# Moving the first small transfers of a decode kernel from SyncE's queue to ScalarE's

## The chip, the cores and the metric

The kernel runs on one core of a Trainium2 chip. The metric is device microseconds (us) of one execution. Before the change three runs took 1076.17, 1074.54 and 1074.22 us; their median is 1074.54 us.

The engines are called as in the profile: PE is TensorE (PEld its weight loads), DVE is VectorE, ACT is ScalarE, POOL is GpSimd, SP is SyncE. Each engine works off its own instructions in order. A transfer from the chip's memory is issued by an instruction on SP or on ACT; each of the two has a queue of transfers of its own (SP's is q1 in the profile, ACT's is q10), and the core's 16 DMA engines serve both.

## The reference

The kernel computes one decode step, for 8 batch rows of width 448, of two attention blocks with two MLP blocks between and behind them:

```python
x = x + A(layernorm(x))     # attention over cached keys and values
x = x + B(layernorm(x))     # MLP block
x = x + A(layernorm(x))     # the same weights and caches again
x = x + B(layernorm(x))

# A: 16 query heads on 8 cached heads, 4096 cached positions, head width 256
q = (x @ wq) as [8, 16, 1, 256]
p = softmax(q @ k^T / 16)
return (p @ v) as [8, 1, 4096] @ wo

# B: with one position only; the shifted groups are zero
x1 = x + shifted(gelu(layernorm(x) @ w1)) @ w2   # = x for one position
return x1 + gelu(layernorm(x1) @ w3) @ w4
```

With a sequence of one position each of the four shifts of `hs` reads only padding, so that part of B adds nothing and w1 and w2 are never loaded. The caches are 8 batch rows x 8 heads x 4096 positions x 256 numbers in bf16, 2 MB for the keys of one row and head and 2 MB for its values: 128 MB of each. They do not fit on the chip and are read for each of the two attention blocks, but for what is kept in between. In all the profile counts 434.18 MB read.

## The kernel before

**Storage.** Keys and values lie in 30 slots of 512 KB (`kv`, `QUARTERS = 30`); one row and head of keys is four units of one slot each. One SP transfer brings one to four consecutive units, that is 512 KB to 2 MB. The weights lie beside them and stay. The 448 rows of `wq` and of `w3` do not divide by 128, so their last 64 rows are folded: `wqx_sb` holds the left half of the columns on partitions 0 to 63 and the right half on partitions 64 to 127 (256 KB each), `w3x_sb` the same for the MLP (112 KB each). The input row lies in `x_row`: the 448 columns, and once more the last 64 of them.

**Work on one row and head.** `front`: PE transposes the keys of each unit (L1510), DVE or ACT moves the result from PSUM back over the keys (L1441, L1442), PE multiplies with the queries (L1406 or L1149), then the softmax. `back`: PE multiplies the probabilities with the values (L1276), DVE splits the sum in two bf16 parts, and PE multiplies with `wo` (L1340). When the last unit of a load has been read, its slots come free.

**Beginning.** `first_queries` transposes the input row on PE (L1600), normalises it (`norm`, L847 and L851 on PE, then a chain on DVE), and multiplies with `wq_sb` and `wqx_sb` (L902 in `q_mms`). Scores of the first head wait for that. The transposes of the first keys do not.

**Loops.** Batch rows run in order; the first attention of row b+1 overlaps the second attention of row b. Keys of five heads and seven value units stay in their slots from the first attention of a row to the second. The MLP of each row (`mid`) stands between its two attentions; that of the first six rows' second block runs once for all of them, that of the last two at the end.

**What sets the order.** All work is first described as operations with their readers and writers (`Plan.op`). `Plan.schedule` then assigns each engine its order by a list scheduling with modelled times: of what is ready, the least `prio` goes first; PE's time depends on how many columns the last window of 3.413 us had (`WIN`, `COLS`), filler matmuls (L1719) are put into gaps of PE from 20 us on. SP's operations go strictly by `prio`; keys and values count up from 0 (`loads`), and a load given `at` gets `4 * at - 0.5`. The planner takes 0.45 us for an issue on SP and starts a transfer 4.0 us after its issue or when the one ahead is done:

```python
free[e] = t + 0.45
start = max(t + self.ISSUE, dma_end)
dma_end = start + o.dur
```

For keys and values it also decides, at that modelled time, which slots are taken and how many units go in one transfer (`next_kv`); single places cap this (`MOST = 1` for the values of three heads of the rows 1 to 7 in the first attention). On ACT a transfer counts 0.1 us and is taken to be there at once. The order and the waits that follow are then written out for each engine; nothing is decided on the chip.

**The first transfers.** On SP: the input row in two pieces (`at` 0), the left half of `wqx` (0.05), the left half of `w3x` (0.06), two key transfers of 2 MB, then `wq` in three pieces of 1 MB (`at` 2), values and keys, `wo`. On ACT: the right halves of `wqx` (L1576) and `w3x` (L1580), then the load of its function table, then nothing until the first eviction.

Of the kernel before, what the change touches and what calls it, by code (L numbers as in the profile page):

```python
# [6 lines left out]
P = 128  # L7
B = 8
D = 448
# [467 lines left out]
def bass_interleave_layers__gqa_block_cached__mixer_s_mlp__decode_kernel(  # L477
# [20 lines left out]
    plan = Plan()  # L498
# [6 lines left out]
    def sb(name, shape, dt):  # L505
        n = 4 if dt in (f32, i32) else 2
        for s in shape[1:]:
            n *= s
        al = 32 if n >= 128 else 8
        cursor[0] = (cursor[0] + al - 1) // al * al  # L510
        t = nc.alloc_sbuf_tensor_at(name, shape, dt, offset=cursor[0], align_bytes=al)
        cursor[0] += (n + al - 1) // al * al
        assert cursor[0] <= high0, (name, cursor[0], high0)
        return t

    wq_sb = sb("wq_sb", [P, 3, 4096], bf)
    wqx_sb = sb("wqx_sb", [P, 2048], bf)
    wo_sb = sb("wo_sb", [P, 32 * D], bf)
    w3_sb = sb("w3_sb", [P, 3, F], bf)
    w3x_sb = sb("w3x_sb", [P, F // 2], bf)  # L520
# [40 lines left out]
    def over(name, shape, dt, at, skip=0):  # L561
        return nc.alloc_sbuf_tensor_at(name, shape, dt, offset=at.manual_sbuf_range[0] + skip)
# [13 lines left out]
    x_row = over("x_row", [B, NC5 * P], bf, w4_sb)  # L576
# [49 lines left out]
    def dma(name, dst, src, nbytes, sem, val, wr, at, row=8192):  # L626

        us = nbytes / 16 / 26.88e3 + nbytes / row / 16 * 0.008
        plan.op("sp", lambda eng: eng.dma_start(dst, src), us / FASTER, name, wr=wr, prio=at,  # L629
                dma=(sem, val))  # L630

    def dma_once(name, parts, keys, at, also=()):

        for i, (dst, src, nbytes, *row) in enumerate(parts):
            dma(name, dst, src, nbytes, nc.alloc_semaphore(f"s_{name}{i}"), 16,
                [keys[i], *(also if i == 0 else ())], 4 * at - 0.5, *row)
# [49 lines left out]
    def const_c(v):  # L686
# [7 lines left out]
            wr=["sel"])  # L694
# [7 lines left out]
    for bank, key in [(psR, "R"), (psM, M)]:  # L702
        plan.op("dve", lambda v, bank=bank: v.memset(bank[:, :], 0.0), 0.5, "const",
                wr=["psM", ("row", 0), ("row", 1)], banks=[key])
# [851 lines left out]
    def second_queries(b, h, prio):  # L1556
# [8 lines left out]
           rd=["psM", ("mom2", b), "cs_q"], wr=[("q2", b % 2, h)], banks=[M], prio=prio)  # L1565


    dma_once("x", [(x_row[:, 0:D], A_x[:, 0, :], 7168), (x_row[:, D + P:], A_x[:, 0, 3 * P:D], 1024)],
             ["xr0", "xr1"], 0)

    def load_wq():
        dma_once("wq", [(wq_sb[:, kc, :], A_wq[kc * P:(kc + 1) * P, :], 1 << 20)
                        for kc in range(3)], ["wq0", "wq1", "wq2"], 2)
        dma_once("wqx", [(wqx_sb[0:64, :], A_wq[384:D, 0:2048], 1 << 19)], ["wqx0"], 0.05)
        s_wqx = nc.alloc_semaphore("s_wqx1")
        plan.op("act", lambda a: a.dma_start(wqx_sb[64:P, :], A_wq[384:D, 2048:4096]), 0.1, "wqx1",  # L1576
                wr=["wqx1"], prio=0, dma=(s_wqx, 16))
        dma_once("w3x", [(w3x_sb[0:64, :], B_w3[384:D, 0:896], 114688)], ["w3x0"], 0.06)
        s_w3x = nc.alloc_semaphore("s_w3x1")
        plan.op("act", lambda a: a.dma_start(w3x_sb[64:P, :], B_w3[384:D, 896:1792]), 0.1, "w3x1",  # L1580
                wr=["w3x1"], prio=1, dma=(s_w3x, 16))

    def load_rest():
        dma_once("wo", [(wo_sb[:, :].rearrange("p (t n) -> p t n", n=2 * D),
# [68 lines left out]
    def with_first_results(k, b):  # L1653
# [15 lines left out]
        run(k[MLP_TO:])  # L1669

    load_wq()
    load_rest()
    first_queries()
# [105 lines left out]
```

## Time and profile before

| | |
|---|---|
| median of three runs | 1074.54 us (1074.22 to 1076.17) |
| the profiled execution | 1071.74 us |
| its span, first to last instruction | 1069.8 us |
| busy: PE, DVE, ACT, POOL | 937.8, 586.8, 345.6, 99.6 us |
| mean granted clock of PE | 0.954 |
| bytes moved, mean rate | 436.39 MB, 408 GB/s |
| first instruction on SP and ACT | 0.72 us |
| first key transfer issued, landed | 2.89, 12.27 us |
| last values landed | 1059.96 us |
| issues of 512 KB: values, keys | 174, 29 |
| issues of 2 MB: values, keys | 61, 66 |

The shares of busy time are means over the span. The page's DMA row shows in tenths how much of each fortieth of the span the 16 DMA engines were in transfer; the GB/s tell how much they moved in it, so that a busy engine with little moved can be seen. "SPq" and "ACTq" are the instructions that issue transfers on the two queues. The chain that ended last is followed back from the last instruction; a DMA piece in it begins at the issue and ends at the landing.

### The profile page before, as it was taken

How to read it: one execution, taken by the hardware profiler on the slowest of the kernel's cores; microseconds unless marked ns; L12 is line 12 of the kernel's file. 1: busy time of each engine (PE TensorE's matmuls, PEld its weight loads, DVE VectorE, ACT ScalarE, POOL GpSimd, SP SyncE). 2: the span in 40 equal slices, each digit the busy share in tenths (PEclk: the TensorE clock that was granted, in tenths of full speed). 3: DMA queues.
4: the chain of work that ended last, by engine and by line, in shares of the span. 5: the costliest groups of instructions: out<-in, count | busy, mean ns of one | idle time of the engine just before them, and what ended most of it. 6: DMA issues, size and time to landing. Idle time of an engine off the chain costs nothing.

```text
span 1069.8 us, 34153 instructions
## 1 busy us (share of the span) xinstructions
PE 937.8 (88%) x15215; PEld 650.7 (61%) x15215; DVE 586.8 (55%) x1879; ACT 345.6 (32%) x946; POOL 99.6 (9%) x284
## 2 busy tenths in 40 slices
PE   4889889998989989988898888898888998998896
PEld 4556556665556656666565565666656675666664
DVE  4345455555555556555565555565555665665464
ACT  1234113341334502354133431344223342253041
POOL 0000000010100101001010100101000000111011
PEclk9899999999999989999999999999999998999896
DMA  9999999999999999999999999999999999999995
GB/s 364 409 425 424 408 391 426 424 422 404 406 427 424 420 396 419 426 426 418 385 424 424 422 403 386 426 425 425 397 402 425 427 419 387 407 425 416 381 422 229
DMA packets 58110, 436.39 MB, mean 408 GB/s; under 512 B 6238, under 2 KB 9452, under 8 KB 35948
## 3 DMA queue, kind: packets, MB, share of 16 engines
q1 hardware_dynamic: 57796, 433.84, 98.6%
q8 instruction: 119, 1.95, 0.7%
q10 hardware_dynamic: 168, 0.38, 0.1%
q14 instruction: 27, 0.22, 0.1%
HBM read 434.18 MB, written 0.01 MB: 406 GB/s over the span
## 4 chain that ended last, share of the span: by engine, by line
DMA 56%; PE 36%; DVE 4%; issue 2%; SPq 1%; ACT 1%; POOL 0%
DMA kv<-in_A_k_cache_dram 30%; DMA kv<-in_A_v_cache_dram 26%; PE psT L1510 11%; PE psP L1276 8%; PE psT L1406 5%; PE psM L1149 3%; PE psM L902 2%; PE psR L1340 2%; PE psP L1719 1%; SPq L629 1%; PE psM L918 1%; DMA w_sb<-in_B_w_dram 1%; DVE oS L1304 1%; DVE oS L1302 1%; PE psP L1312 1%
## 5 line engine op out<-in xcount | busy, mean ns | idle before, releaser
L1510 PE MATMUL psT<-ident_f,kv 128*128 128x128 f32 x2752 | 372.7, 282 | 27.9 <-DMA kv<-in_A_k_cache_dram 26.2
L1510 PEld LDWEIGHTS psT<-ident_f,kv 128*128 128x128 f32 x2752 | 301.5, 143 | 107.6 <-issue 56.6
L1441 DVE COPY kv<-psT 128x512 f32<-128x512 f32 x364 | 250.4, 691 | 186.4 <-PE psT L1510 179.2
L1442 ACT COPY kv<-psT 128x512 f32<-128x512 f32 x356 | 207.9, 586 | 376.3 <-PE psT L1510 300.3
L1276 PE MATMUL psP<-kv,pT 128*2 128x256 bf16 x4032 | 170.9, 281 | 26.3 <-DMA kv<-in_A_v_cache_dram 24.3
L1406 PE MATMUL psT<-kv,qz 128*32 128x512 bf16 x1664 | 134.2, 396 | 3.8 <-ACT kv L1442 1.9
L1276 PEld LDWEIGHTS psP<-kv,pT 128*2 128x2 bf16 x4032 | 82.8, 82 | 68.8 <-DMA kv<-in_A_v_cache_dram 32.6
L1229 POOL PARTITION_ALL_REDUCE gm<-pm x128 | 45.4, 355 | 772.3 <-DVE pm L1227 762.2
L1239 ACT ACTIVATE pT<-sS,nb,fac 128x32 bf16<-128x32 bf16 x128 | 52.6, 417 | 122.7 <-DVE nb L1233 122.7
L1302 DVE CAST oS<-psP 128x256 bf16<-128x256 f32 x126 | 53.2, 422 | 51.0 <-PE psP L1276 49.9
L1340 PE MATMUL psR<-wo_sb,oT 128*1 128x448 bf16 x444 | 64.0, 372 | 7.7 <-DVE oT L1319 3.0
L1243 POOL PARTITION_ALL_REDUCE Db<-rs x128 | 51.0, 398 | 179.1 <-ACT pT L1239 179.1
L1719 PE MATMUL psP<-ident_f 128*128 128x256 bf16 x370 | 59.7, 288 | 0.0
L1312 PEld LDWEIGHTS psP<-sel,oS 128*128 128x128 bf16 x504 | 23.1, 98 | 60.1 <-DVE oS L1304 56.3
L1239 ACT ACTIVATE pT<-sS,nb 128x32 bf16<-128x32 bf16 x128 | 40.7, 326 | 54.7 <-DVE nb L1233 54.7
L1312 PE MATMUL psP<-sel,oS 128*128 128x2 bf16 x504 | 31.5, 166 | 30.2 <-DVE oS L1304 29.0
L1406 PEld LDWEIGHTS psT<-kv,qz 128*32 128x32 bf16 x1664 | 34.2, 95 | 37.3 <-issue 12.8
L1421 DVE CAST sr<-psT 128x512 bf16<-128x512 f32 x54 | 37.3, 691 | 33.5 <-PE psT L1406 33.4
L1304 DVE TENSOR_TENSOR oS<-psP,oS 128x256 bf16<-128x256 f32 x126 | 53.3, 423 | 2.8
L1149 PE MATMUL psM<-qz,kv 128*128 128x48 bf16 x1344 | 47.6, 186 | 6.4 <-issue 4.2
L1149 PEld LDWEIGHTS psM<-qz,kv 128*128 128x128 bf16 x1344 | 41.4, 99 | 17.2 <-issue 10.6
L1222 DVE CAST sS<-psM 128x64 bf16<-128x64 f32 x128 | 28.1, 219 | 41.3 <-PE psM L1149 28.4
(197 smaller groups left out, 796.5 us busy)
## 6 DMA issues: line engine op xcount, KB each, us to landing
kv<-in_A_k_cache_dram SPq DMA_DIRECT2D x66, 2048.0 KB, 23.2
kv<-in_A_v_cache_dram SPq DMA_DIRECT2D x61, 2048.0 KB, 17.3
kv<-in_A_v_cache_dram SPq DMA_DIRECT2D x174, 512.0 KB, 8.2
kv<-in_A_k_cache_dram SPq DMA_DIRECT2D x16, 1024.0 KB, 9.6
kv<-in_A_k_cache_dram SPq DMA_DIRECT2D x29, 512.0 KB, 9.0
kv<-in_A_k_cache_dram SPq DMA_DIRECT2D x9, 1536.0 KB, 17.4
kv<-in_A_v_cache_dram SPq DMA_DIRECT2D x13, 1024.0 KB, 9.2
kv<-in_A_v_cache_dram SPq DMA_DIRECT2D x4, 1536.0 KB, 11.0
```

Of the source, the lines that this page charges most:

```text
L1149: last = t.matmul(ps[:, SB + 2 * i:SB + 2 * i + 2 * REP], a()[:, c:256:2], bcast(rhs(c), REP, 1), start=(c == 0), stop=(c == 1))
L1239: return a.activation(pT[nr][:, :, :].rearrange("p i j -> p j i")[:, jj, :], sview[:, jj, :], ACT.Exp, bias=nb[nm][:, jj:jj + 1], scale=sc ...
L1276: last = t.matmul(ps[g4:g4 + 2, PV0:PV0 + DH], pT[nr][:, k, :], slot_ap(q, s * 256, 256), start=(i < 4), stop=(i >= 28), skip_group_check= ...
L1302: plan.op("dve", lambda v: v.tensor_copy(oS[:, 0, :], po), 0.36, "o", rd=[("pv", par, x) for x in range(4)], wr=["oS0"], banks=[bk], prio=hi)
L1304: plan.op("dve", lambda v: v.tensor_tensor(oS[:, 1, :], po, oS[:, 0, :], ALU.subtract), 0.36, "o", rd=["oS0"] + [("pv", par, x) for x in r ...
L1312: last = t.matmul(ps[:, PV1 + 2 * c:PV1 + 2 * c + 2], oS[:, w, c:DH:2], sel[:, :], start=(w == 0), stop=(w == 1))
L1340: last = t.matmul(psR[r:r + 1, 0:D], oT[no][:, i % 2, i // 2:i // 2 + 1], wo_sb[:, a:a + D], start=(k == 1 and i < 2), stop=(k == turn_at ...
L1406: last = t.matmul(psT[bank][32 * g:32 * g + 32, :], qz[:, a:a + 32], slot_ap(qs[g // 2], g % 2 * 1024, 1024)[:, c:1024:2], start=(half == ...
L1441: return e.tensor_copy(dst, psT[bank][:, :])
L1442: return e.copy(dst, psT[bank][:, :])
L1510: last = t.transpose(psT[bank][:, s * P:(s + 1) * P], src, ident_f[:, :])
L1719: return t.matmul(dst, ident_b, bcast(ident_b[:, 0:n // 4], 4, 1), start=True, stop=True)
```

## The change

The four small transfers of SP go to ACT, through a helper that describes an ACT operation with a semaphore of its own. All six have the least `prio` on ACT and go in the order in which they are described: the two pieces of the input row, the right half of `wqx`, its left half, the left half of `w3x`, its right half. SP's first operation is then the first keys. `wq`, `wo`, `w3`, `w4` and all keys and values stay on SP. What is moved, to where, and the arithmetic stay as they are.

```diff
-    dma_once("x", [(x_row[:, 0:D], A_x[:, 0, :], 7168), (x_row[:, D + P:], A_x[:, 0, 3 * P:D], 1024)],
-             ["xr0", "xr1"], 0)
+    def by_act(key, dst, src):
+
+        sem = nc.alloc_semaphore(f"s_{key}")
+        plan.op("act", lambda a: a.dma_start(dst, src), 0.1, key, wr=[key], prio=0, dma=(sem, 16))
+
+    by_act("xr0", x_row[:, 0:D], A_x[:, 0, :])
+    by_act("xr1", x_row[:, D + P:], A_x[:, 0, 3 * P:D])
 
     def load_wq():
         dma_once("wq", [(wq_sb[:, kc, :], A_wq[kc * P:(kc + 1) * P, :], 1 << 20)
                         for kc in range(3)], ["wq0", "wq1", "wq2"], 2)
-        dma_once("wqx", [(wqx_sb[0:64, :], A_wq[384:D, 0:2048], 1 << 19)], ["wqx0"], 0.05)
-        s_wqx = nc.alloc_semaphore("s_wqx1")
-        plan.op("act", lambda a: a.dma_start(wqx_sb[64:P, :], A_wq[384:D, 2048:4096]), 0.1, "wqx1",
-                wr=["wqx1"], prio=0, dma=(s_wqx, 16))
-        dma_once("w3x", [(w3x_sb[0:64, :], B_w3[384:D, 0:896], 114688)], ["w3x0"], 0.06)
-        s_w3x = nc.alloc_semaphore("s_w3x1")
-        plan.op("act", lambda a: a.dma_start(w3x_sb[64:P, :], B_w3[384:D, 896:1792]), 0.1, "w3x1",
-                wr=["w3x1"], prio=1, dma=(s_w3x, 16))
+        by_act("wqx1", wqx_sb[64:P, :], A_wq[384:D, 2048:4096])
+        by_act("wqx0", wqx_sb[0:64, :], A_wq[384:D, 0:2048])
+        by_act("w3x0", w3x_sb[0:64, :], B_w3[384:D, 0:896])
+        by_act("w3x1", w3x_sb[64:P, :], B_w3[384:D, 896:1792])
```

## The prediction

> **What bounds the kernel now.** I read the profile's page first, for the busy shares and the chain that ended last; then the stretches (busy time, granted clock, DMA share and GB/s between two times), then the order of time on SP's queue, then the chain's beginning and end.
>
> The page: the two lines under the slices, the first queue, the shares of the chain, and from the DMA issues the two kinds that carry most of the stream.
> ```profile
> PE 937.8 (88%) x15215; PEld 650.7 (61%) x15215; DVE 586.8 (55%) x1879; ACT 345.6 (32%) x946; POOL 99.6 (9%) x284
> DMA  9999999999999999999999999999999999999995
> q1 hardware_dynamic: 57796, 433.84, 98.6%
> DMA 56%; PE 36%; DVE 4%; issue 2%; SPq 1%; ACT 1%; POOL 0%
> ...
> kv<-in_A_k_cache_dram SPq DMA_DIRECT2D x66, 2048.0 KB, 23.2
> ...
> kv<-in_A_v_cache_dram SPq DMA_DIRECT2D x174, 512.0 KB, 8.2
> kv<-in_A_k_cache_dram SPq DMA_DIRECT2D x16, 1024.0 KB, 9.6
> kv<-in_A_k_cache_dram SPq DMA_DIRECT2D x29, 512.0 KB, 9.0
> ```
> SP's queue is in transfer for 98.6% of the span, and the slices show nine tenths or more everywhere but in the last. TensorE is at 88%, but its work hangs on what lands. So the time is: when the stream starts, how fast it runs, and what is left to do after its last byte.
>
> The stretches. The columns are start:end, length, busy time of the five rows, granted clock, DMA share, GB/s.
> ```profile
> 0.00:2.00 2.00, 0.00 (x0) 0.00 (x0) 1.04 (x3) 0.04 (x1) 1.29 (x21) 1.00 0.02 4
> 2.00:5.00 3.00, 0.27 (x5) 0.21 (x5) 1.18 (x10) 1.25 (x1) 0.29 (x1) 1.00 0.90 229
> 5.00:8.00 3.00, 1.12 (x36) 1.03 (x36) 1.62 (x11) 0.00 (x0) 0.00 (x0) 1.00 1.06 350
> 8.00:28.00 20.00, 12.52 (x150) 10.80 (x151) 6.94 (x14) 2.93 (x5) 0.00 (x0) 0.97 1.01 427
> ...
> 260.00:284.00 24.00, 21.59 (x542) 14.01 (x544) 13.38 (x67) 4.13 (x14) 1.86 (x5) 1.00 1.01 391
> ...
> 1058.00:1070.00 12.00, 6.49 (x211) 5.64 (x207) 4.63 (x23) 0.23 (x1) 1.68 (x6) 0.50 0.04 13
> ```
> Three things to see: the opening, 2 to 5 us, moves 229 GB/s where the steady stream moves 427; a stretch of many 512 KB issues (15 of them are issued in 260 to 284) moves 391; and 10 to 12 us of work are left when the stream is over.
>
> SP's queue in order of time, and the first and the last transfer of the chain:
> ```profile
> 0.72 0.75 SPq L629 DMA_DIRECT2D x_row<-in_A_x_dram  x2
> 1.51 0.56 SPq L629 DMA_DIRECT2D wqx_sb<-in_A_wq_dram  x1
> 2.12 0.73 SPq L629 DMA_DIRECT2D w3x_sb<-in_B_w_dram  x1
> 2.89 1.24 SPq L646 DMA_DIRECT2D kv<-in_A_k_cache_dram  x2
> 4.17 1.92 SPq L629 DMA_DIRECT2D wq_sb<-in_A_wq_dram  x3
> ```
> ```profile
> 2.89 9.38 DMA kv<-in_A_k_cache_dram
> ...
> 1038.96 21.00 DMA kv<-in_A_v_cache_dram
> ```
> The chain begins with the four small issues on SP (0.72 to 2.85 us) and then the first keys, issued at 2.89, landed at 12.27. Nothing ahead of them holds them but SP's own issuing.
>
> **The change part by part.** *SP.* Four issues go: two of the input row (0.75 us together), one of the query weights (0.56), one of the MLP weights (0.73), with the gaps 2.17 us. The first keys can be issued at 0.72, and everything behind them (the three wq issues at 4.17, wo at 8.03) moves up with them.
>
> *What that gives the stream.* The bytes stay, so what counts is how much fuller the opening gets. At 427 GB/s three microseconds move 1.281 MB; 2 to 5 us moved 0.687, which is 0.594 MB or 1.39 us short; 5 to 8 us moved 1.050, 0.54 us short. If the keys filled both, the stream would be 1.93 us ahead; that is the upper end, below the 2.17 us of issuing. The lower end is 0: the DMA share in the opening is already 0.90, and if the engines are really full with small rows, keys beside them only swap places. A loss by slower interleaving is not excluded; no row shows two queues full at once, so I bound it by as much the other way as the 5 to 8 us shortfall, 0.54 us. I take 1.4 us: the first 3 us filled, the keys' own run-up of 0.54 us kept. The first bytes cannot come earlier than now: the earliest issue is at 0.72 in both, and the first 2 us move 4 GB/s. I lean to the upper half since wo's rows of 1792 bytes, as short as those of w3x, moved 379 and 381 GB/s in the stretches 44 to 48 and 48 to 52 us, while wo was landing; short rows alone do not make 229. What is missing in the opening is work in flight.
>
> *ACT.* It issues six transfers in place of two: at 0.57 and 0.61 us each from its two rows, 2.3 us more. Behind them waits its table load (1.28 us, now at 1.97, then at about 4.3). Its first real work is an eviction at 16.03, some 14.6 after the shift, so 9 us of cover.
>
> *The input row.* It is first on ACT as it was first on SP: issued from 0.72 on, two issues of 0.57 in place of 0.40 and 0.28, so about 0.4 us later, and its bytes share the engines with 4 MB of keys. TensorE's queue has its transposes (4.69 us) and the first layer norm's matmuls (to 6.35) ahead of the first key transposes at 12.31. With the keys at 10.9 the row may land 4.5 us later before it holds anything; the two folded loads that share the queue now landed in 3.6 and 4.5 us after issue. Cost 0. VectorE's chain on it (to 8.85) serves the query matmuls at 25.7, which wait for wq.
>
> *The halves of wqx and w3x.* On ACT behind the row. First used at 25.7 and 118.8 us: cost 0, cover over 15 us.
>
> *wq.* It lands at 25.5 by its 15.5 to 20.2 us from issue, in line behind the keys; it comes earlier by what the stream gains. Between 22.95 and 25.70 TensorE waits. By the planner's rule no filler matmul is placed before 20 us of its clock, and its clock now has this wait earlier, so some of the five fillers at 21.66 go. The 128 query matmuls (3.49 us in the chain) already run at a clock of 0.69 and 0.50; a microsecond more here would be hidden: SP's key issue of 11.80 hangs for 34 us because its queue is full, and wo is landing until 54.6, so the stream does not thin out.
>
> *The planner.* The kernel's order is computed by a list scheduler before the launch, from modelled times, so the move re-plans everything. By its own figures the keys' transfer began at 6.35 us (four issues of 0.45, 4.0 to start, 1.19 for wqx0, which it counts as 512 KB, 0.26 for w3x0) and now begins at 4.0: 2.35 us earlier. A plain shift would leave the order. What does not shift is its clock's fixed 3.413-us windows, which make matmuls cheap or dear, and the 20-us rule. Ties will fall otherwise, slots come free in another order, and the SP issues are merged or split otherwise. Price: 260 to 284 us moved 391 where 427 is steady, 24 x (1 - 391/427) = 2.02 us for 15 issues of 512 KB, 0.135 us each. Check by the whole: 436.39 MB at 427 take 1022 us, the stream runs from 2 to 1060, 36 us lost, less 1.9 of the opening, over 203 such issues: 0.17 each. How many change no row says. 84 of the 203 are forced (value loads of three heads in seven batch rows are capped at one unit), 4 more by the last head and 8 by kept units; some 107 are free. I take 0 change as the centre and 30 either way as ends (a quarter of the free ones): plus or minus 4.1 us.
>
> *Sum.* -1.4 (stream) + 0 + 0 + 0 + 0 (plan). The profiled execution took 1071.74 us (span 1069.8, 1.94 around it) and becomes 1070.3; the median of the three runs is 1074.54, 2.8 above it, and becomes **1073.1**.
>
> **The rivals.**
> *No gain: the engines were full.* The first keys are issued 2.17 us earlier and land when they did, since the small rows take the same engine time beside them as ahead of them. For it: the share of 0.90. Against it: 229 GB/s. The time: 1074.5. [...]
>
> *Slower: the new plan splits more loads.* The place is SP's issues after 50 us, the price 0.135 us per extra 512 KB issue. From 11 extra issues on the gain is gone; from 27 on it is over 0.2% slower; with 30, 1073.1 + 4.1 = 1077.2. For it: the kernel carries many constants (lags, caps, due times) that fit one order of events. Against it: two thirds of the stream is in issues that the shift leaves alone.
>
> *Faster: the plan merges more.* The same mechanism the other way; with 15 fewer issues 2.0 us less, 1071.1.
>
> *The row comes late.* If its packets wait behind the keys for more than 4.5 us, TensorE, whose queue has the row's transposes first, holds the key transposes. At a landing of 9 us, as 512 KB key issues have, it would be 0.72 + 9 against 4.66 + 4.5: 0.6 us, 1073.7. It is inside the forecast's own range.
>
> **How the numbers follow.** Forecast (stream gain, plan about as good): 0.42, with its own range 1071.5 to 1075.0. No gain: 0.15. Plan worse: 0.25. Plan better: 0.18. A measurement of this kernel tells about 0.2%, 2.15 us, from no change: faster is below 1072.4, slower above 1076.7. Faster: 0.16 of the better plan and a quarter of the forecast (0.10), 0.26. Slower: 0.23 of the worse plan and 0.01 of the rest, 0.24. Within 0.2%: 0.50. The range takes in the worse plan a little past its 30 issues and the better one to 23 fewer (1073.1 - 3.1): 1070.0 to 1078.5, with a tenth left out at each end.
>
> **What would show it.** SP's first key issue at 0.72 and six issues on ACT; 2 to 5 us near 427 GB/s in place of 229; the first key transposes at about 10.9 in place of 12.31, and the query matmuls at about 24.3; the row's transposes before 9 us; the count of 512 KB issues near 203; the last values landing near 1058.5 and the same 10 us behind them. Wrong: keys landing at 12.3 (no gain), another count of 512 KB issues, a stretch where DMA share falls below 0.9 that had none, or an end after the last values that is longer than 10 us.

## The result

The changed kernel takes 1077.02 us (median of 22 runs, 1074.1 to 1081.33) against 1074.28 us of the kernel before (22 runs, 1071.74 to 1078.06). The ratio is 1.0028, with a 95% interval of 1.0016 to 1.0039: slower by 0.28%, some 3 us, where 1.4 us faster was forecast. The time lies in the stated range. Single executions of one kernel spread over 6 to 7 us, and the profiled execution of before, 1071.74 us, is the fastest of its 22. So later stages of two profiles are not compared one against one below; the opening is, since it repeats within about a microsecond (at 28 us the changed kernel is 2.8 and 1.8 us behind in its two profiled executions, the old order with the new queues 1.9 and 2.2).

The page of the changed kernel, with the busy row, the DMA and GB/s rows of the slices, the two queues and the shares of the chain:
```profile
PE 939.6 (87%) x15194; PEld 654.5 (61%) x15194; DVE 595.2 (55%) x1892; ACT 335.5 (31%) x933; POOL 99.6 (9%) x284
...
DMA  9999999999999999999999999999999999999995
GB/s 320 409 427 422 408 397 425 425 421 404 413 423 427 415 393 418 424 426 415 383 424 423 426 405 354 427 424 426 412 405 424 425 419 384 407 425 415 362 423 231
...
q1 hardware_dynamic: 57172, 433.45, 98.5%
...
q10 hardware_dynamic: 360, 0.76, 0.2%
...
DMA 58%; PE 35%; DVE 3%; issue 2%; ACT 1%; SPq 1%
```
The bytes are the same and DMA is as busy as before. The first of the GB/s numbers is the one to see: 320, where the page of before has 364. A slice is 26.9 us long, and the moved transfers lie in the first.

SP's queue of the changed kernel in order of time:
```profile
0.72 0.87 SPq L646 DMA_DIRECT2D kv<-in_A_k_cache_dram  x2
1.64 1.66 SPq L629 DMA_DIRECT2D wq_sb<-in_A_wq_dram  x3
```
and its opening in stretches (start:end, length, busy time of five rows, granted clock, DMA share, GB/s):
```profile
0.00:2.00 2.00, 0.00 (x0) 0.00 (x0) 1.04 (x3) 0.00 (x0) 1.28 (x21) 1.00 0.57 102
2.00:5.00 3.00, 0.00 (x0) 0.00 (x0) 0.82 (x6) 0.73 (x1) 0.29 (x1) 1.00 0.76 289
5.00:8.00 3.00, 0.04 (x2) 0.07 (x3) 0.00 (x0) 0.56 (x1) 0.00 (x0) 1.00 1.03 370
8.00:20.00 12.00, 7.90 (x83) 6.99 (x84) 7.23 (x26) 0.98 (x2) 0.00 (x0) 1.00 0.99 296
20.00:28.00 8.00, 2.75 (x24) 1.79 (x22) 2.08 (x3) 1.36 (x3) 0.00 (x0) 0.96 1.04 419
```
The same two last stretches of the kernel before:
```profile
8.00:20.00 12.00, 7.48 (x46) 7.03 (x47) 5.30 (x12) 2.35 (x4) 0.00 (x0) 1.00 1.00 423
20.00:28.00 8.00, 5.04 (x106) 3.77 (x105) 1.63 (x3) 0.59 (x1) 0.00 (x0) 0.92 1.03 432
```
The keys are issued at 0.72 as forecast, and the first 8 us move more than before. Then, from 8 to 20 us, the engines are in transfer all the time (0.99) and move 296 GB/s; the kernel before moves 423 there. The lines of transfers to landing name what is still under way; first the changed kernel, then the kernel before:
```profile
wqx_sb<-in_A_wq_dram ACTq DMA_DIRECT2D x2, 256.0 KB, 13.3
w3x_sb<-in_B_w_dram ACTq DMA_DIRECT2D x2, 112.0 KB, 17.8
```
```profile
wqx_sb<-in_A_wq_dram ACTq DMA_DIRECT2D x1, 256.0 KB, 3.6
wqx_sb<-in_A_wq_dram SPq DMA_DIRECT2D x1, 256.0 KB, 4.5
w3x_sb<-in_B_w_dram ACTq DMA_DIRECT2D x1, 112.0 KB, 3.8
w3x_sb<-in_B_w_dram SPq DMA_DIRECT2D x1, 112.0 KB, 4.4
```
The two halves of w3x, 112 KB each, land 17.8 us after their issue, at about 21 us; before, the four halves took 3.6 to 4.5 us. The slow stretch ends when they are through.

Stretch by stretch, rate times length gives the bytes moved by 28 us: 10.28 MB before (8 + 687 + 1050 + 423 x 12 + 432 x 8 KB), 9.09 MB after. At 427 GB/s the difference is 2.8 us. "Ahead" and "behind" below are this number; it stays between 2.2 and 2.9 us behind up to 500 us. The first key transposes start at 10.95 us (12.31 before), but those of the second keys wait 2.50 us for their landing at 18.91, and the query matmuls start at 27.88 in place of 25.70. In order of time on PE:
```profile
18.91 1.31 PE L1510 MATMUL psT<-ident_f,kv 128*128 128x128 f32 x10 [2.50 <-DMA kv<-in_A_k_cache_dram]
...
27.88 0.22 PE L902 MATMUL psM<-yb,wq_sb 128*128 128x8 bf16 x3 [4.55 <-issue]
```
The end is as it was: the last values land at 1065.20 of a span of 1075.1, 9.9 us behind them, as before.

### The profile page after: what moved, and what is told of

Same layout as the page of the kernel before. It is cut to its first block, busy times and chain, and to the rows that moved or that the text cites. A ratio compares the mean times of both kernels' runs of the same rounds, so it can differ in the third digit from the quotient of the medians.

```text
span 1075.1 us, 34089 instructions
## 1 busy us (share of the span) xinstructions
PE 939.6 (87%) x15194; PEld 654.5 (61%) x15194; DVE 595.2 (55%) x1892; ACT 335.5 (31%) x933; POOL 99.6 (9%) x284
## 4 chain that ended last, share of the span: by engine, by line
DMA 58%; PE 35%; DVE 3%; issue 2%; ACT 1%; SPq 1%
DMA kv<-in_A_k_cache_dram 30%; DMA kv<-in_A_v_cache_dram 27%; PE psT L1510 13%; PE psP L1276 7%; PE psT L1406 5%; PE psM L1149 3%; PE psM L902 2%; PE psR L1340 2%; PE psP L1720 1%; PE psM L918 1%; DVE oS L1304 1%; DVE oS L1302 1%; PE psP L1312 1%; DVE kv L1441 1%; PE psM L1066 1%
## 5 line engine op out<-in xcount | busy, mean ns | idle before, releaser
L1510 PE MATMUL psT<-ident_f,kv 128*128 128x128 f32 x2752 | 377.9, 285 | 31.6 <-DMA kv<-in_A_k_cache_dram 30.1
L1510 PEld LDWEIGHTS psT<-ident_f,kv 128*128 128x128 f32 x2752 | 306.8, 144 | 110.6 <-issue 53.4
L1441 DVE COPY kv<-psT 128x512 f32<-128x512 f32 x384 | 263.6, 691 | 197.3 <-PE psT L1510 189.5
L1442 ACT COPY kv<-psT 128x512 f32<-128x512 f32 x336 | 196.0, 586 | 365.8 <-PE psT L1510 290.6
L1720 PE MATMUL psP<-ident_f 128*128 128x256 bf16 x346 | 56.5, 290 | 0.0
```

The source lines that it names most:

```text
L1441: return e.tensor_copy(dst, psT[bank][:, :])
L1442: return e.copy(dst, psT[bank][:, :])
L1510: last = t.transpose(psT[bank][:, s * P:(s + 1) * P], src, ident_f[:, :])
L1720: return t.matmul(dst, ident_b, bcast(ident_b[:, 0:n // 4], 4, 1), start=True, stop=True)
```

## The experiments

Each ratio below is that of a run to the kernel before, timed on the same chip. Two theories stand at first. Q: the loss is made in the opening, by a second queue beside the keys. P: it is made by the new order that the planner finds. To part them, the runs take the planner's order of one kernel and then move only the small transfers between the queues, by a helper behind the planning (`small` holds the operations by their keys; the lines that fill it are left out here):

```diff
     plan.schedule()
+
+    def place(eng, keys, at):
+
+        ops = [small[k] for k in keys]
+        for o in ops:
+            plan.order[o.eng].remove(o)
+            o.eng = eng
+        plan.order[eng][at:at] = ops
+        for order in plan.order.values():
+            for i, o in enumerate(order):
+                o.pos = i
```

**The old order with the new queues** (edit of the kernel before):
```diff
+    place("act", ["xr0", "xr1", "wqx1", "wqx0", "w3x0", "w3x1"], 0)
     plan.synchronise()
```


> Every engine keeps the order that the planner made for the kernel before; only the six small transfers are then taken out of it and put at the head of ACT's queue, as in the changed kernel. Theory Q (the loss is made in the opening, by two queues sharing the engines): 8 to 20 us run near 300 GB/s as in the changed kernel, the stream is about 2.8 us behind the kernel before at 28 us and stays so, time 2.8 us above the kernel before (ratio 1.0026). Theory P (the loss is the new order after 50 us, the opening's loss is caught up): ratio 1.000, within 0.1%.

Measured: ratio 1.0024 (1.0011 to 1.0036), 1.9 us behind at 28 us. 8 to 20 us:
```profile
8.00:20.00 12.00, 8.04 (x79) 7.31 (x77) 6.73 (x21) 2.35 (x4) 0.00 (x0) 1.00 1.01 324
```
The order of all engines is the old one, and most of the loss is there. Q holds for this part.

**The new order with the old queues** (edit of the changed kernel):
```diff
+    place("sp", ["xr0", "xr1", "wqx0", "w3x0"], 0)
+    place("act", ["wqx1", "w3x1"], 0)
     plan.synchronise()
```


> The planner's order of the changed kernel, with the six transfers put back on the queues and in the order of the kernel before. Theory Q: 2 to 28 us as in the kernel before (427 GB/s from 8 us on), ratio 1.000 within 0.1%. Theory P: ratio 1.0028.

Measured: the opening is that of the kernel before (0.2 us behind at 28 us), but the ratio is 1.0025 (1.0012 to 1.0038).
```profile
8.00:20.00 12.00, 7.31 (x46) 6.54 (x47) 6.32 (x14) 1.71 (x3) 0.00 (x0) 1.00 0.99 419
```
So the new order costs too; Q alone, which expected 1.000, is not the whole.

**Why a second queue holds the keys up.** Two forms of Q were put against each other. Q1: any row on the second queue costs the engines a fixed time. Q2: rows that all go to partitions 0 to 63, or all to 64 to 127, hold up the keys that go to that side. Both are guesses of the author's. The run that parts them keeps queues, rows and bytes and spreads each half over all 128 partitions; by Q1 that changes nothing, by Q2 the stream comes back:
```diff
-(wqx_sb[0:64, :], A_wq[384:D, 0:2048], 1 << 19)
+(wqx_sb[0:P:2, :], A_wq[384:D, 0:2048], 1 << 19)
-a.dma_start(wqx_sb[64:P, :], A_wq[384:D, 2048:4096])
+a.dma_start(wqx_sb[1:P:2, :], A_wq[384:D, 2048:4096])
 (the same for w3x_sb)
+    place("act", ["xr0", "xr1", "wqx1", "wqx0", "w3x0", "w3x1"], 0)
```


> As the first, but each folded half is written to every second partition (0, 2, ... 126 and 1, 3, ... 127) in place of partitions 0 to 63 and 64 to 127; rows, bytes and packets are the same, the weights land on wrong partitions. [...] Q1 (each row on the second queue costs the engines a fixed time beside a full first queue): unchanged, near 300 GB/s from 8 to 20 us, 2.8 us behind at 28 us. [...]

Measured: 8 to 20 us at 413 GB/s in place of 324, 1.1 us ahead at 28 us (10.77 MB), 1074.15 us in its one run.
```profile
2.00:5.00 3.00, 0.00 (x0) 0.00 (x0) 1.18 (x10) 0.73 (x1) 0.29 (x1) 1.00 0.88 322
5.00:8.00 3.00, 0.92 (x29) 0.86 (x30) 0.18 (x1) 0.55 (x1) 0.00 (x0) 1.00 1.00 415
8.00:20.00 12.00, 11.05 (x78) 9.62 (x76) 8.03 (x23) 2.93 (x5) 0.00 (x0) 1.00 1.00 413
```
Only the partitions that the rows go to differ from the first run, and 3 us of stream come back. Q1, a fixed price for any row, falls: it matters which partitions the rows go to, as Q2 has it. The two queues between 8 and 20 us (packets, MB, share of the time of the 16 engines), in the changed kernel, in this run and in the kernel before, show where the time goes:
```profile
q1 hardware_dynamic: 258, 2.95, 81.9%
q10 hardware_dynamic: 258, 0.60, 17.5%
```
```profile
q1 hardware_dynamic: 464, 4.40, 88.4%
q10 hardware_dynamic: 272, 0.56, 12.1%
```
```profile
q1 hardware_dynamic: 472, 5.08, 100.1%
```
The halves themselves (q10) take little. It is SP's queue that has 82% of the engines' time in the changed kernel and moves only 2.95 MB in it: 300 GB/s of its own time, against 415 with the halves spread and 423 before. In the packet records of these three traces a row of 16 KB takes, in the mean from 8 to 20 us, 0.90, 0.64 and 0.62 us. The one-sided rows make the rows beside them slow.

What these runs show is the partitions: 324 GB/s with each half on one side, 413 with the halves spread. Whether it is the keys of the same side that are held up, and by what, they do not show.

The same kernel, timed; by Q2 the gain is there again:

> The kernel of the all-partitions run once more, timed (order of the kernel before, all six transfers on ACT, the folded halves on every second partition, so on wrong ones). [...] If that run was a chance: ratio 1.002, behind at 28 us.

Measured: 1073.1 us, ratio 0.9990 (0.9977 to 1.0003), 1.0 us ahead at 28 us. Against the first run (1.0024) that is 0.34%, 3.6 us, for 2.8 us of stream.

**A second queue of long, full-width rows** (edit of the kernel before):
```diff
+    place("act", ["wq0", "wq1", "wq2"], 2)
     plan.synchronise()
```


> The order of the kernel before with its small transfers where they were; the three 1 MB pieces of wq (128 rows of 8 KB each, 24 rows for each of 16 engines) go on ACT behind them, so that a second queue of about as many rows, over all 128 partitions, runs beside the keys. Q1: 8 to 20 us well under 427 GB/s (300 to 360), at least 2.5 us behind at 28 us. Q2: no loss, within 0.5 us of the kernel before at 28 us.

Measured: 0.7 us behind at 28 us, 1075.88 us in one run.
```profile
8.00:20.00 12.00, 2.63 (x13) 2.63 (x14) 2.09 (x7) 0.00 (x0) 0.00 (x0) 1.00 1.01 417
```
The 384 rows of 8 KB on the second queue leave the stream at 417 GB/s. The 0.7 us are lost before 12 us; SP's halves meet wq now and take 5.5 and 7.8 us to land in place of 4.5 and 4.4. It is a little over what Q2 allowed, and far from Q1's 2.5.

**Only the row on ACT, the halves in line behind the keys** (edit of the kernel before):
```diff
+    place("act", ["xr0", "xr1"], 0)
+    place("sp", ["wqx1", "wqx0"], 6)
+    place("sp", ["w3x0", "w3x1"], 30)
```


> Order of the kernel before. Only the input row is on ACT; SP begins with the keys and has the two halves of wqx behind wq, those of w3x behind w3. Q2: nothing runs beside the keys but 16 short rows, so the opening is full and the stream about 1.3 us ahead at 10 us; the halves then pass one after the other in line at about half the rate, which costs up to 1.2 us for wqx near 28 us and 0.5 us for w3x near 120 us. At 28 us between 0.1 and 1.3 us ahead; ratio 0.999 to 1.000. If any second queue at the start holds the keys up (Q1): behind at 10 us.

Measured: 1.3 us ahead at 20 us, 0.6 behind at 28 us; ratio 1.0017 (1.0002 to 1.0032), worse than expected.
```profile
8.00:20.00 12.00, 10.80 (x97) 8.71 (x95) 8.09 (x23) 2.93 (x5) 0.00 (x0) 1.00 1.00 423
20.00:28.00 8.00, 2.48 (x94) 2.52 (x94) 0.00 (x0) 0.00 (x0) 0.00 (x0) 0.63 1.05 333
...
102.00:122.00 20.00, 15.66 (x284) 11.69 (x282) 10.78 (x30) 5.84 (x19) 2.27 (x6) 0.98 1.02 391
```
With no halves beside them the first keys run as forecast, and the row alone on ACT does no harm. The halves take their toll where they pass: 20 to 28 us move 333 GB/s (432 before), 1.9 us for 512 KB; 102 to 122 us move 391 (415 before), 1.1 us for 224 KB. Both are more than the expectation's half rate would cost (1.2 and 0.5 us); that rate was an estimate of the author's, and the reading nearest to it is the 229 GB/s, of 427, of the kernel before from 2 to 5 us. It needs no second queue. No run has the spread halves in line, but the packet records speak against the shortness of the rows: a 4 KB row of the halves takes 0.31 us there, a 4 KB row of a full-width 512 KB load 0.16, and the 16 KB rows from 20 to 28 us take 0.73 in place of 0.62.

**The part of the change that leaves the two sides on two queues** (edit of the kernel before):
```diff
+    place("act", ["xr0", "xr1"], 2)
     plan.synchronise()
```


> Order of the kernel before; the one part of the change that leaves the two sides of the folded halves on two queues: wqx1 and w3x1 first on ACT as before, then the input row; SP begins with wqx0 and w3x0, then the keys, 0.75 us earlier than before. Q2: the two sides go at the same time and are through before most of the keys, so no loss: 0.3 to 0.8 us ahead at 28 us, ratio 0.9993 within 0.1%. Q1: the rows of the row and of w3x1 meet the keys: no gain or a loss of up to 0.5 us.

Measured: 1071.92 us, ratio 0.9984 (0.9969 to 0.9999), 0.4 us ahead at 28 us.
```profile
2.00:5.00 3.00, 0.00 (x0) 0.00 (x0) 1.19 (x10) 1.28 (x1) 0.29 (x1) 1.00 0.90 251
5.00:8.00 3.00, 0.00 (x0) 0.00 (x0) 0.00 (x0) 0.00 (x0) 0.00 (x0) 1.00 1.09 413
8.00:20.00 12.00, 9.51 (x93) 8.28 (x93) 7.22 (x23) 2.35 (x4) 0.00 (x0) 1.00 0.99 419
```
Only the row is moved, behind the halves on ACT; the keys are issued at 1.99, and both sides are filled at the same time, mostly ahead of them. It is the fastest of the timed versions, though its interval ends just below 1; of its gain of about 1.7 us the opening explains 0.4, the rest is inside the interval.

**What the order costs.** The planner's constant for the start of a transfer was changed in the kernel before, so that it finds a third order while queues and first transfers stay:
```diff
-    ISSUE, LEAD = 4.0, 5.0
+    ISSUE, LEAD = 2.8, 5.0
```


> The kernel before with one constant of the planner changed (a transfer is taken to start 2.8 us after its issue in place of 4.0); queues and first transfers are as before, the order after 50 us is re-planned, by a shift about half as large as the change makes. Theory P1 (the constants fit the old order, so another order costs): ratio 1.002 to 1.004, like the run with the new order on the old queues (1.0025). P2 (each order is a draw, as often better as worse): anything from 0.998 to 1.003. P3 (orders are alike, that run was chance): 1.000 within 0.1%.

Measured: 1.0026 (1.0011 to 1.0041), with an opening like that of before (0.1 us behind at 28 us). A second re-planning, and again a cost on the old queues. Both orders have 199 issues of 512 KB where the old one has 203, so the count of short issues, which the prediction priced, is not what costs.

Whether the new order also costs behind its own opening was asked by three runs on one chip: the changed kernel with spread halves, the changed kernel, and the old order with the new queues.

> The changed kernel, order and queues as they are, with the folded halves on every second partition (the wrong ones). From the runs so far the opening is worth -1.1 us against the kernel before. If the new order itself costs 2.5 us, as it did on the old queues: ratio 1.0014. If the new order costs nothing behind its own opening, and the changed kernel is slower by its opening alone: 0.9990.

Measured: 1.0000 (0.9986 to 1.0014), 1.2 us ahead at 28 us; between the two expectations.

> The changed kernel beside the run that has its queues and the old order, on one chip. If its loss is the opening alone: both 1.0025, within 0.1% of each other. If the new order costs 2.5 us on top: this one 1.0045, 0.2% above the other.

Measured: 1.0033 (1.0020 to 1.0046), 1.8 us behind at 28 us.

> The old order with the changed kernel's queues once more: 1.002 to 1.0025; 8 to 20 us near 310 GB/s, 1.9 to 2.8 us behind at 28 us.

Measured: 1.0020 (1.0006 to 1.0035), 2.2 us behind at 28 us, 8 to 20 us at 314 GB/s. The changed kernel is 0.13% above it, again between its two expectations (within 0.1%, or 0.2%).

Ratio to the kernel before, by order and by where the six transfers go:

| transfers | old order | new order |
|---|---|---|
| queues of before | 1 | 1.0025 |
| all on ACT, halves on one side each | 1.0024, 1.0020 | 1.0028, 1.0033 |
| all on ACT, halves spread | 0.9990 | 1.0000 |

Down the columns, halves on one side against halves spread are 0.28 to 0.34% apart, 3.0 to 3.7 us, with either order. Along the rows with all six on ACT the new order costs 0.04, 0.13 and 0.10%, about 1 us, and 0.25% on the old queues; the intervals of each are wide enough for one cost of 0.1 to 0.2% in all of them. So of the 3.0 to 3.5 us the opening makes about 2.4 (the mean of the two runs with the old order), and the order about 1. That the order costs is shown on the old queues; on the new ones its size is not settled, nor is the place in the 1000 us behind the opening, since the stretches there scatter by a microsecond or two between executions.

## Why the prediction was wrong

- **What bounds the kernel: right.** A microsecond of stream lost in the opening stayed lost: within one order the ratios follow the microseconds ahead or behind at 28 us.
- **SP's issues: right. The first transposes at 10.9: right by luck.** The keys are issued at 0.72, and the first transposes start at 10.95. But the keys came by another way than forecast: with the halves spread the transposes start at 8.9 to 9.6, and the one-sided halves hold them back to where the forecast had them.
- **ACT: right.** Its table load starts at 4.27 (about 4.3 was forecast), and its first eviction at 15.85 does not wait for it.
- **What that gives the stream: wrong, the step that failed.** It was taken as 1.4 us gained, with 0.54 us as the most that could be lost, "by slower interleaving". The gain is there for as long as the step looked: 1.0 us ahead at 8 us, and 1.0 to 1.2 us at 28 us with the halves spread. Its parts are others than forecast: the first 2 us, which were to move no more than before, move 102 GB/s in place of 4 (0.5 us), and 2 to 5 us move 289 and not nearly 427 (0.4 us of the 1.39). What the step did not see is that the halves, once beside 2 MB transfers, pass slowly (until 21 us instead of 6.5) and that all this time they hold the keys back: 3.9 us lost between 8 and 24 us. The bound of 0.54 us came from a row, 5 to 8 us, in which the halves were ending and the first keys starting; it said nothing of the two kinds side by side for 12 us, and should have been left as open as it was.
- **The reading of 229 GB/s: half right.** It was put down to too little in flight, on the ground that wo's equally short rows run at 380. In part it was: with the halves behind the keys, 2 to 5 us move 290. That it is not 427 even then goes with a DMA share of 0.72 in that stretch: the keys are only starting, which the step allowed for in 5 to 8 us alone. And wo's rows go to all 128 partitions, those of the halves to 64: the row that was compared was short in the same way, not narrow in the same way. What the narrowness made of the 229 in the kernel before, no run shows.
- **The halves cost nothing: wrong in kind.** As forecast, no reader waits for them. What they cost is paid by the other transfers: on a full queue 512 KB on one side at a time cost 1.9 us, 224 KB 1.1 us.
- **The input row: right.** Its transposes start at 7.96 us in place of 4.69, later than the 0.4 us said, but inside the 4.5 us of cover, and no key transpose waits for it. The 3.6 and 4.5 us that the prediction read for two loads sharing one queue are those of wqx's halves, one on each queue; the two on SP's took 4.5 and 4.4.
- **The query matmuls at about 24.3: wrong.** They start at 27.88: the last piece of wq lands 24.8 us after its issue (20.2 before), in the slow stream. It is the same cause; in the changed kernel with spread halves they start at 24.16.
- **The plan: centre of 0 wrong, ends right, mechanism wrong.** Two re-planned orders cost 0.25% on the old queues, well inside the 4.1 us either way; but there are four fewer issues of 512 KB, not more. (The range's upper end, 1078.5, is at 0.135 us each 40 more issues, not "a little past" 30.)
- **The rivals.** The time went to the side of the slower one, but mostly by a mechanism that was not listed. "The engines were full" fell: with the halves spread the opening gains 1.0 to 1.2 us. The plan that is worse has its part, about 1 us, but not by the price that was set on it.

## What to carry to other kernels

Before a small transfer is moved beside a large stream, look at which partitions it writes: here those that filled partitions 0 to 63 or 64 to 127 alone slowed what flowed with them (8 to 20 us at 296 to 324 GB/s, 413 with the same rows over all 128). Let such transfers pass when little else is under way, as at the start of the kernel before (there they land 3.6 to 4.5 us after their issue), or lay the data out over all 128 (ratio 0.9990 in place of 1.0024). Price a transfer by what it does to the others in flight, not only by who waits for it. Where an order is planned from modelled times, test a move once with the order held, since the re-planning can be worth as much as the move (here 1.0025 for the order alone, 1.0024 for the queues alone).

## What the runs showed of the hardware

Beside a queue of 2 MB transfers with rows of 16 KB, a second queue with rows of 4 KB and 1.8 KB moves on slowly: 0.75 MB took until about 21 us. From 8 to 20 us the trace has 258 packets of each queue, and with the halves spread 464 of SP's and 272 of ACT's; why the second lags, no run shows. With the rows over all partitions w3x still takes 14.2 us to land, but the stream stays at 413 GB/s: here being slow did not hurt, being one-sided did.

The one-sided rows are at most 0.75 MB of the 3.6 to 3.9 MB that pass from 8 to 20 us, and take 17.5% of the engines' time in the changed kernel. The stream falls to 296 to 324 GB/s because the long rows beside them take longer, 0.90 us in place of 0.62. By what the one kind slows the other is left open; no run shows it.
